# Second batch's attention scores: one float32 product becomes three products of float32r parts, and the parts get single buffers

## The chip, the core and the metric

The program runs on one core of one Trainium2 chip. The metric is the device time of one execution in microseconds (us). Five engines work side by side, each on its own queue of instructions in order: TensorE (PE; its weight loads are listed as PEld), VectorE (DVE), ScalarE (ACT), GpSimd (POOL) and SyncE (SP), which issues most of the transfers. PE runs at one of two granted clocks, 1.2 or 2.4 GHz; the views give the granted share (0.5 or 1.0, or a mean between them).

## The reference, cut to what matters

```python
scores = scale * np.matmul(q, k.transpose(0, 1, 3, 2))     # 4 batches x 12 heads, 448 x 448, depth 64
scores = np.where(mask, -1000000000.0, scores)             # causal
attn = exp(scores - max); attn = attn / (sum(attn) + 1e-9)
x = (attn @ v).transpose(0, 2, 1, 3).reshape(1792, 768)
h = np.maximum(np.maximum(x @ w1, x @ w2), x @ w3)         # first mixture
x = h @ w_out
# then a top-1 mixture of 8 experts: out[token] = gate * relu(x @ w1[e]) @ w2[e]
```

Everything is float32. The choice of an expert by the largest logit depends on the result of the attention, and that is why large products are made from float32r parts: a float32r copy ("high part") of each operand and the float32r rest ("low part"), with the three products high-high, low-high and high-low summed in PSUM.

## The kernel before

Attention works on units. A unit is a pair of heads of one batch, so that six units make a batch: units 0 to 5 are the first batch, 6 to 11 the second, and so on. A unit's queries and keys are transposed so that depth lies on the partitions, the two heads on partitions 0 to 63 and 64 to 127. A block is 112 rows of queries. Since the mask is causal, block i needs 112 * (i + 1) columns of scores: 112, 224, 336 or 448.

The first batch is computed alone (`first_heads`). The second batch is computed in pieces inside `first_mixture`, a loop of 36 steps (m = 0 to 35). In each step, half of one weight tile of the first mixture is decoded from float64 words and split, and nine matmuls of the mixture for the first batch run (`h_half`, L674). The order of the instructions is written out by hand there (`manual_schedule`), so each engine takes its instructions in the order of the program text. One step does this:

- `w_split`: ACT copies the high part of a decoded weight (wp, L649), POOL subtracts the low part (L650), and the pair goes to memory.
- `next(st)`: one piece of the second batch's attention, see below.
- `w_decode`: ACT runs L159 and L160, DVE runs L165, L166 and L167, POOL runs L170.
- `run(late)`: copies and small operations that `next(st)` left for later.
- `h_max` in every second step (ACT L683 or L688, DVE L685 and L689), then `h_half` on PE.

A unit of the second batch takes six steps: three parts p (p = 0 has the blocks of 112 and 224 columns, p = 1 the block of 336, p = 2 the block of 448), two steps each. In a part's first step, `nat_d` multiplies the previous part's probabilities by the values (PE, L332), and `nat_b` takes row maxima and masks (DVE, L301) and the exponential (ACT, L305), for both heads. In its second step, `nat_c` transposes the probabilities (PE, L312) and copies them to SBUF (nh: ACT L318, but DVE L317 for the second head of p = 0), and `nat_a` makes the next part's scores (PE, L284). In the second step of p = 1, `nat_t` also transposes the queries and keys of the next unit (PE, L269); the copies to SBUF (qt by ACT, L271; kt by DVE, L273) are late operations of that step, and stand ahead of the nh copies. The order in that step is thus: PE transposes q and k, transposes the probabilities, makes the scores of p = 2 of the present unit from the present qt and kt; then the next qt and kt are written.

Before the change, qt and kt of even units lie in the buffers with the tags qh and kh, those of odd units in ql and kl. A unit's copies therefore never wait for the unit before. The first of the six transposes of the second batch (unit 6) is made at the end of `first_heads`, where the four buffers are free. The third and fourth batch use the same four tags for their own float32r parts (`at_t`, `at_qk`), with the three products that the change brings to the second batch.

The scores of the second batch are made with float32 operands: each product shows in the trace as two matmul instructions. The two heads' products stand on different rows of the array.

Of the kernel before, what the change touches and what calls it, by code (L numbers as in the profile page):

```python
# [11 lines left out]
F32 = mybir.dt.float32  # L12
F32R = mybir.dt.float32r
# [3 lines left out]
AF = mybir.ActivationFunctionType  # L17
ALU = mybir.AluOpType
# [5 lines left out]
def f32(ap):  # L24
    return ap.bitcast(F32)
# [7 lines left out]
def kernel(  # L33
# [15 lines left out]
    nc = tc.nc  # L49
    P = 128  # L50
    B, H, S, D = q.shape
    NP = H // 2
    CP = 112
# [12 lines left out]
    SCALE = 1.0 / math.sqrt(D)  # L66
# [13 lines left out]
    def prio(n):  # L80
# [13 lines left out]
    att = ph_a.enter_context(tc.tile_pool(name="att", bufs=2))  # L94
# [14 lines left out]
        out=mask[:, S - CP :], in_=mask[:, S - CP :], compare_op=ALU.is_ge, fill=BIG, base=0,  # L109
# [121 lines left out]
    M = [slice(0, D), slice(D, 2 * D)]  # L231
# [19 lines left out]
    NPC = 3  # L251
    qk_t, n_sc, n_pt, n_pth, n_bm = {}, {}, {}, {}, {}

    def blocks(n):
        return ((0, 1), (2,), (3,))[n % NPC]
# [4 lines left out]
    def nat_t(u):  # L260

        rq, rk_ = raws.pop((u, "q")), raws.pop((u, "k"))
        qt, kt = (att.tile([P, S], F32, tag=t + "hl"[u % 2], name=f"{t}t{u}", bufs=1) for t in "qk")
        qk_t[u] = (qt, kt)
        late = []
        for nm, r in (("q", rq), ("k", rk_)):
            pq = ps_t.tile([P, 512], F32, tag="pst", name=f"p{nm}{u}")
            for c in range(NC):
                nc.tensor.transpose(pq[:, c * CP : (c + 1) * CP], r[:, c].rearrange("p j d -> p (j d)"), ident[:CP, :CP])  # L269
            if nm == "q":  # L270
                late.append(lambda pq=pq: nc.scalar.activation(qt, pq[:, :S], AF.Copy, scale=-SCALE))  # L271
            else:
                late.append(lambda pq=pq: nc.vector.tensor_copy(kt, pq[:, :S]))  # L273
        return late

    def nat_a(n):

        qt, kt = qk_t[n // NPC]
        ss = [ps_t.tile([P, 512], F32, tag="pst", name=f"sn{n}_{j}") for j in range(2)]
        off = 0  # L280
        for i in blocks(n):
            L = CP * (i + 1)
            for j, m in enumerate(M):
                nc.tensor.matmul(  # L284
                    ss[j][:CP, off : off + L], lhsT=qt[m, CP * i : CP * i + CP], rhs=kt[m, :L], start=True, stop=True
                )
            off += L
        n_sc[n] = ss

# [62 lines left out]
    def nat_steps():  # L352

        n0, n1 = NPC * NP, NPC * NN
        for n in range(n0, n1):
            u, p = divmod(n, NPC)
            late = []
            if n > n0:
                late += nat_d(n - 1)
            nat_b(n, 0)  # L360
            nat_b(n, 1)
            if p == 2:

                late.append(lambda: at_load(u + 3, "qk") if u + 1 < NN else None)
                late.append(lambda: at_load(u + 1, "v"))
            yield late
            late = []
            if p == 1 and u + 1 < NN:
                late += nat_t(u + 1)
            late += nat_c(n, 0) + nat_c(n, 1)  # L370
            if n + 1 < n1:
                nat_a(n + 1)
            yield late
        yield nat_d(n1 - 1)
# [361 lines left out]
    def first_heads():  # L736
# [9 lines left out]
        for u in range(NP):  # L746
            if u:
                at_p(u - 1, 1, PB[0] + PB[1])
            at_qk(u)
            at_e(u, 0)  # L750
            st = w_decode(u)
            w_raw(u + 2)
            at_e(u, 1, st)
            drain(st)
            if u:
                at_av(u - 1, 1)
                at_x(u - 1, 1)
                at_load(u + 1, "v")
            at_p(u, 0, PB[0] + PB[1])
            at_load(u + 2, "qk")  # L760
            if u + 1 < NP:
                at_t(u + 1)
            else:
                run(nat_t(NP))
            at_n(u)
            if u == 0:
                warm(6)
            at_av(u, 0)
            if u:
                x_split(u - 1)  # L770
            at_r(u)
            at_x(u, 0)
        at_p(NP - 1, 1, PB[0] + PB[1])
        w_split(0)
        nat_a(NPC * NP)
        at_av(NP - 1, 1)
        at_x(NP - 1, 1)
# [71 lines left out]
    def iota_f(shape, pattern, name, base=0, cm=0):  # L849
# [17 lines left out]
        out=tri, in_=tri, compare_op=ALU.is_gt, fill=0.0, base=0, pattern=[[1, P]], channel_multiplier=-1  # L867
# [473 lines left out]
```

## Time and profile before

| | us |
|---|---|
| median of 3 runs | 956.46 |
| lowest and highest | 954.72, 957.21 |
| the profiled execution | 959.22 |
| its span on the core | 957.5 |
| the second batch's scores on PE, first and last start | 79.3 to 204.8 |

Times of rows are microseconds from the start of the span; mean durations marked ns are nanoseconds. The profiled execution took 2.76 us more than the median; 1.7 us of its time lie around the span. The profile gives busy time and share of each engine, a chain of the work that ended last, and for each idle stretch of an engine what ended it. The release of a wait is inferred from semaphore events.

### The profile page before, as it was taken

To read this page: it belongs to the slowest core of one execution; us is meant where nothing else is said; L and a number is where in the kernel's file an instruction comes from. 1 tells how busy PE (TensorE), PEld (TensorE's weight loads), DVE (VectorE), ACT (ScalarE), POOL (GpSimd) and SP (SyncE) were. 2 spreads that over 40 slices of the span, in tenths; PEclk is the share of its full clock that TensorE was granted. 3 is DMA by queue.
4 is the path that set the end of the run, shared out by engine and by line. 5 is a ranking of instruction groups with operands and counts; after the bars stand their busy time and mean duration, and the time that the engine had idled before them with its cause. 6 is when DMAs were issued, how large, how long until landed. Compare 5 with 4: busy or idle time off the path is not lost.

```text
span 957.5 us, 17073 instructions
## 1 busy us (share of the span) xinstructions
PE 929.2 (97%) x5500; PEld 825.3 (86%) x5500; DVE 486.0 (51%) x1287; ACT 458.1 (48%) x1037; POOL 166.9 (17%) x186
## 2 busy tenths in 40 slices
PE   8888999999999999999999998999999999999997
PEld 5666888788989999999999897989989998998996
DVE  4665777866765645455554214541211217749244
ACT  6776667655654656565531003142212216757253
POOL 0114555552321110001020000010010010100101
PEclk9998999999999999999999999899999999999999
DMA  6336787876555532264452992191011116949410
GB/s 147 91 90 199 243 251 247 261 237 184 175 167 160 151 105 63 71 174 147 146 167 83 362 319 80 59 337 38 35 55 46 34 50 223 354 130 382 147 34 26
DMA packets 126354, 150.10 MB, mean 157 GB/s; under 512 B 75934, under 2 KB 93342, under 8 KB 126240
## 3 DMA queue, kind: packets, MB, share of 16 engines
q1 hardware_dynamic: 123200, 135.37, 45.2%
q0 software_dynamic: 3040, 13.41, 4.0%
q8 instruction: 46, 0.75, 0.3%
q14 instruction: 68, 0.56, 0.2%
HBM read 129.85 MB, written 26.77 MB: 164 GB/s over the span
## 4 chain that ended last, share of the span: by engine, by line
PE 85%; DVE 8%; ACT 4%; issue 1%; DMA 1%; POOL 1%; SPq 0%; POOLq 0%; ACTq 0%; DVEq 0%
PE pm L674 24%; PE po L1235 16%; PE ph L1216 16%; PE py L713 9%; PE ss L452 3%; PE pp L511 3%; PE av L547 3%; PE av L535 2%; PE an L332 2%; PE pht L1227 2%; DVE pt L466 1%; PE pxt L1152 1%; ACT pt L471 1%; PE sn L284 1%; PE pr L486 1%
## 5 line engine op out<-in xcount | busy, mean ns | idle before, releaser
L674 PE MATMUL pm<-xh,wp 128*128 128x448 f32 x864 | 272.0, 378 | 0.1
L674 PEld LDWEIGHTS pm<-xh,wp 128*128 128x128 f32 x864 | 162.9, 189 | 23.6 <-issue 10.2
L674 PE MATMUL pm<-xl,wp 128*128 128x448 f32 x432 | 158.8, 368 | 0.0
L1235 PE MATMUL po<-w2h,th 128*128 128x384 f32 x288 | 100.2, 348 | 0.0
L1235 PE MATMUL po<-w2l,th 128*128 128x384 f32 x288 | 97.2, 337 | 0.0
L1235 PE MATMUL po<-w2h,tl 128*128 128x384 f32 x288 | 96.9, 337 | 0.0
L1230 DVE TENSOR_TENSOR tl<-pht,th 128x512 fp32r<-128x512 f32 x36 | 24.9, 690 | 135.1 <-ACT th L1229 88.5
L471 ACT ACTIVATE pt<-pt,bm 112x224 f32<-112x224 f32 (+3 forms) x144 | 75.0, 522 | 26.0 <-DVE bm L466 24.7
L674 PEld LDWEIGHTS pm<-xl,wp 128*128 128x128 f32 x432 | 81.9, 190 | 5.7 <-issue 0.3
L1216 PE MATMUL ph<-w1h,xh 128*128 128x512 f32 x216 | 86.4, 400 | 0.0
L1216 PE MATMUL ph<-w1h,xl 128*128 128x512 f32 x216 | 85.1, 394 | 0.0
L1216 PE MATMUL ph<-w1l,xh 128*128 128x512 f32 x216 | 84.8, 393 | 0.0
L1244 POOL DMA_INDIRECT out_dram<-os,six x18 | 18.4, 1020 | 283.1 <-ACT os L1243 170.9
L466 DVE CUSTOM_DVE_ANT_0 pt<-ss,mask 112x224 f32<-112x224 f32 (+3 forms) x144 | 58.7, 445 | 15.2 <-PE ss L452 11.7
L713 PE MATMUL py<-woh,hth 128*128 128x400 f32 (+1 forms) x168 | 60.6, 360 | 3.6 <-ACT ys L722 3.6
L685 DVE TENSOR_TENSOR g<-pm,g 128x448 f32<-128x448 f32 x48 | 29.8, 620 | 58.3 <-PE pm L674 57.8
L713 PE MATMUL py<-wol,hth 128*128 128x400 f32 (+1 forms) x168 | 58.5, 348 | 0.0
L713 PE MATMUL py<-woh,htl 128*128 128x400 f32 (+1 forms) x168 | 58.4, 347 | 0.0
L1221 ACT ACTIVATE h__7114<-ph 128x512 f32<-128x512 f32 x36 | 21.6, 600 | 70.5 <-PE ph L1216 70.5
L1235 PEld LDWEIGHTS po<-w2h,tl 128*128 128x128 f32 x288 | 54.2, 188 | 0.8
L1235 PEld LDWEIGHTS po<-w2h,th 128*128 128x128 f32 x288 | 54.1, 188 | 0.7
L1235 PEld LDWEIGHTS po<-w2l,th 128*128 128x128 f32 x288 | 54.0, 188 | 0.0
(273 smaller groups left out, 1804.3 us busy)
## 6 DMA issues: line engine op xcount, KB each, us to landing
wp<-wpdram SPq DMA_DIRECT2D x108, 384.0 KB
w1r<-in_moe_w_dram SPq DMA_DIRECT2D x42, 512.0 KB
w2r<-in_moe_w_dram SPq DMA_DIRECT2D x56, 384.0 KB
wpdram<-wp SPq DMA_DIRECT2D x36, 384.0 KB
wxh<-in_moe_w_dram SPq DMA_DIRECT2D x24, 384.0 KB
qraw<-in_q_dram SPq DMA_DIRECT2D x48, 112.0 KB
kraw<-in_k_dram SPq DMA_DIRECT2D x48, 112.0 KB
vraw<-in_v_dram SPq DMA_DIRECT2D x48, 112.0 KB
```

Source lines behind the costliest of these rows:

```text
L452: nc.tensor.matmul(ss, lhsT=l[m, qc], rhs=r[m, :L], start=n == 0, stop=n == len(prods) - 1)
L466: nc.vector.tensor_tensor_reduce(out=pr, in0=ss, in1=mask[:, S - L :], scale=1.0, scalar=3.0e38, op0=ALU.add, op1=ALU.min, accum_out=bm[:, ...
L471: nc.scalar.activation(pr, pr, AF.Exp, bias=bm[:, i : i + 1], scale=-1.0, accum_out=sm[:, j, i : i + 1])
L511: nc.tensor.transpose(pp[:CP, off : off + CP], pt[:, POFF[i] + kt * CP : POFF[i] + (kt + 1) * CP], ident[:CP, :CP])
L547: nc.tensor.matmul(av[:, CP * kt : S], lhsT=vs[:, j, kt, :], rhs=src[:, PTOFF[kt] : PTOFF[kt] + L], start=kt == 0 and src is pth, stop=kt ...
L674: nc.tensor.matmul(pm[:, :S], lhsT=l[:, kk % 3, :], rhs=r, start=kk == 0 and c == 0, stop=kk == KD - 1 and c == 2)
L685: nc.vector.tensor_max(gs["g"], pm[:, :S], gs["g"])
L713: nc.tensor.matmul(pm[:, :w], lhsT=l[:, kk, cs], rhs=r[:, kk, c0 : c0 + w], start=kk == 0 and c == 0, stop=kk == KF - 1 and c == 2,)
L1216: nc.tensor.matmul(pm[a], lhsT=l[:, kk], rhs=r[kk][:, cs], start=kk == 0 and c == 0, stop=kk == KD - 1 and c == 2)
L1221: nc.scalar.activation(h_[:, 512 * a : 512 * a + 512], pm[a], AF.Relu)
L1230: nc.vector.tensor_sub(tl[:, kr], pt, f32(th[:, kr]))
L1235: nc.tensor.matmul(po[a][:, :HN], lhsT=l[:, kk], rhs=r[kk][:, HN * a : HN * a + HN], start=kk == 0 and c == 0, stop=kk == KF2 - 1 and c == 2,)
```

## The change

`nat_t` makes four tiles in place of two: float32r high parts (qh, kh) and low parts (ql, kl) of the scaled queries and the keys. ACT writes qh and then kh; DVE writes ql from the transposed queries and qh, and kl from the transposed keys and kh. Each of the four tags has one buffer, which every unit uses. `nat_a` makes each block's scores with three products per head, summed in PSUM.

```diff
-        qt, kt = (att.tile([P, S], F32, tag=t + "hl"[u % 2], name=f"{t}t{u}", bufs=1) for t in "qk")
-        qk_t[u] = (qt, kt)
+        qh, ql, kh, kl = (att.tile([P, S], F32R, tag=t, name=f"{t}n{u}", bufs=1) for t in ("qh", "ql", "kh", "kl"))
+        qk_t[u] = (qh, ql, kh, kl)
...
-            if nm == "q":
-                late.append(lambda pq=pq: nc.scalar.activation(qt, pq[:, :S], AF.Copy, scale=-SCALE))
-            else:
-                late.append(lambda pq=pq: nc.vector.tensor_copy(kt, pq[:, :S]))
+            def parts(nm=nm, pq=pq):
+                if nm == "q":
+                    nc.scalar.activation(qh, pq[:, :S], AF.Copy, scale=-SCALE)
+                    nc.vector.scalar_tensor_tensor(
+                        out=ql, in0=pq[:, :S], scalar=-SCALE, in1=f32(qh), op0=ALU.mult, op1=ALU.subtract
+                    )
+                else:
+                    nc.scalar.copy(kh, pq[:, :S])
+                    nc.vector.tensor_sub(kl, pq[:, :S], f32(kh))
+
+            late.append(parts)
...
-        qt, kt = qk_t[n // NPC]
+        qh, ql, kh, kl = qk_t[n // NPC]
...
-            for j, m in enumerate(M):
-                nc.tensor.matmul(
-                    ss[j][:CP, off : off + L], lhsT=qt[m, CP * i : CP * i + CP], rhs=kt[m, :L], start=True, stop=True
-                )
+            for c, (l, r) in enumerate(((qh, kh), (ql, kh), (qh, kl))):
+                for j, m in enumerate(M):
+                    nc.tensor.matmul(
+                        ss[j][:CP, off : off + L], lhsT=l[m, CP * i : CP * i + CP], rhs=r[m, :L], start=c == 0,
+                        stop=c == 2,
+                    )
```

## Rows read from the trace of the kernel before

**Rows 1.** The page: busy us of each engine (share of span) xinstructions.
```profile
PE 929.2 (97%) x5500; PEld 825.3 (86%) x5500; DVE 486.0 (51%) x1287; ACT 458.1 (48%) x1037; POOL 166.9 (17%) x186
```
**Rows 2.** Windows, one unit: busy us of PE, PEld, DVE, ACT, POOL; clock; DMA.
```profile
134.84:156.91 22.07, 20.95 (x138) 17.79 (x138) 17.05 (x51) 14.91 (x34) 12.17 (x12) 1.00 0.79 246
```
**Rows 3.** PE's waits, 64 to 222: us in total, times, longest.
```profile
PE an L332 <- DVE nh L317: 5.0, 4, 1.6
```
**Rows 4.** The chain of waits from 130 to 160: start, us, what.
```profile
...
134.84 0.43 DVE nh L317
...
135.31 1.20 PE an L332 x10
...
139.75 0.94 PE sn L284 x4
...
146.48 0.76 PE sn L284 x8
...
153.24 0.80 PE sn L284 x4
...
154.07 0.51 ACT wp L649
...
156.91 0.43 DVE nh L317
...
```
**Rows 5.** The timeline of ACT: start, us, operation, [idle before, releaser].
```profile
...
139.31 0.52 ACT L271 ACTIVATE qt<-pq 128x448 f32<-128x448 f32 x1
139.73 0.76 ACT L318 COPY nh<-pn 112x336 f32<-112x336 f32 x2
...
142.73 1.23 ACT L305 ACTIVATE nt<-nt,nm 112x448 f32<-112x448 f32 x2 [1.83 <-DVE nm L301]
...
153.60 0.56 ACT L688 CAST hth<-g 128x448 fp32r<-128x448 f32 x1 [2.18 <-DVE g L685]
...
```
**Rows 6.** The timeline of DVE, in two units.
```profile
...
97.22 0.62 DVE L273 COPY kt<-pk 128x448 f32<-128x448 f32 x1
97.95 0.62 DVE L301 CUSTOM_DVE_ANT_0 nt<-sn,mask 112x448 f32<-112x448 f32 x1
...
141.54 0.62 DVE L273 COPY kt<-pk 128x448 f32<-128x448 f32 x1
142.07 0.62 DVE L301 CUSTOM_DVE_ANT_0 nt<-sn,mask 112x448 f32<-112x448 f32 x1
...
```
**Rows 7.** The third and fourth batch's parts: count, ns min/median/max, starts, forms.
```profile
...
L421 DVE SCALAR_TENSOR_TENSOR ql<-pq,qh x12: 616/625/625, 222.7 to 458.1; 128x448 fp32r<-128x448 f32 x12
...
L430 ACT CAST kh<-pk x12: 524/529/547, 222.6 to 458.0; 128x448 fp32r<-128x448 f32 x12
L431 DVE TENSOR_TENSOR kl<-pk,kh x12: 614/615/619, 223.3 to 458.7; 128x448 fp32r<-128x448 f32 x12
...
```
**Rows 8.** The timeline of PE, the third batch's scores from three products.
```profile
...
243.73 0.30 PE L452 MATMUL ss<-kh,qh 64*112 64x112 f32 x2
...
244.42 0.32 PE L452 MATMUL ss<-kh,qh 64*112 64x336 f32 x2
...
244.88 0.36 PE L452 MATMUL ss<-kh,qh 64*112 64x448 f32 x2
...
245.28 0.37 PE L452 MATMUL ss<-kl,qh 64*112 64x448 f32 x2
245.58 0.47 PE L674 MATMUL pm<-xh,wp 128*128 128x448 f32 x1
...
```
**Rows 9.** Window of the clock (columns as rows 2), PE's timeline, and the chain.
```profile
91.00:95.00 4.00, 4.00 (x17) 3.74 (x18) 2.74 (x11) 3.61 (x8) 2.22 (x3) 0.58 1.05 373
...
90.99 1.55 PE L332 MATMUL an<-vraw,nh 112*112 112x65 f32 x10 [1.63 <-DVE nh L317]
...
96.98 0.94 PE sn L284 x4
...
```
**Rows 10.** PE's timeline near the end of the second batch.
```profile
...
207.67 1.39 PE L332 MATMUL an<-vraw,nh 112*112 112x65 f32 x12 [0.31 <-ACT nh L318]
...
```

## The prediction, as it was made before the changed kernel ran

> **What bounds the kernel now.** I read the page first [rows 1]: PE is busy 97% of the span, so work taken off PE should count. But that share is a mean over stages, so I looked at the stage the change is in, 79 to 215 us, by windows. A unit of the second batch repeats every 22.07 us, and PE is busy 20.95 us of that [rows 2]: it idles 1.1 us per unit. Next, PE's own waits over the stage [rows 3]: nearly all of that idle time is one wait, by the product with the values (L332) for DVE's copy nh (L317), four times with 5.0 us in total (units 6, 8, 9 and 10). So something other than PE sets the period.
>
> The chain of waits [rows 4] must be read with care here. It runs from DVE's nh at 134.84 along PE to the scores that end at 154.04, jumps to ACT's copy wp at 154.07, and comes back by DVE to nh at 156.91. The jump is a coincidence of 0.03 us: ACT's timeline shows L688 started at 153.60 [rows 5], and 0.47 us from one ACT start to the next is what ACT takes between such copies when it waits for nothing (139.31 to 139.73 is 0.42 [rows 5]). L688 itself waited for DVE. Following ACT and DVE alone, I find each DVE instruction either straight behind the one before it or behind ACT, and each ACT idle stretch ended by DVE: DVE's L301 behind kt at once, 0.53 us after it [rows 6], and ACT's exponential after 1.83 us of waiting for L301 [rows 5]. So DVE and ACT, each in its own order and waiting for each other, form a loop of 22.07 us that PE does not enter. PE is some 1.1 us shorter and waits for the loop once per unit.
>
> **The change, part by part.**
>
> *Scores on PE.* Per unit they now take 0.76 (p = 0), 0.80 (p = 1) and 0.94 us (p = 2) of the chain [rows 4], together 2.50. The three products need no guess, as the third batch makes the same blocks with them [rows 8]: blocks 112 and 224 take 243.73 to 244.42 = 0.69, block 336 takes 0.46, block 448 to the next matmul 0.70. The last pair of 448 takes 0.30 us to the next matmul where 0.20 lies between the earlier ones ((245.28 - 244.88) / 2), so leaving the half-array products costs 0.10. The second batch leaves them three times: 0.79 + 0.56 + 0.70 = 2.05. PE saves 0.45 us a unit (0.24 of it in p = 2), 2.7 us over six units.
>
> The Trainium skill, "FP8 and Floating Point Precision", section TensorE Precision Notes, says that true FP32 takes four passes through the array. By that rule three products would take 3/4 of 2.50 and save 0.63 us a unit, 3.8 in all; the trace shows two matmul instructions for a float32 product, and the third batch's rows give the smaller 0.45.
>
> *Copies.* ACT: qt becomes qh (same size), and kh is added, 0.53 us, 0.42 from start to start. DVE: kt (0.62) goes, ql and kl come, 0.62 each [rows 7]; from start to start DVE needs 0.53 [rows 6]. Loop cost: 0.53 us on DVE per unit, unless something else is later.
>
> *Single buffers.* This is the new wait. qh of the next unit may be written only when p = 2 of the present unit is through PE, because its products read qh. ACT has it first in that step's late work; behind it in ACT's order stand kh, two nh copies and wp, behind ql on DVE stand kl and then L301. In the unit of [rows 4] the p = 2 scores end at 140.69, and 0.24 sooner after the change: 140.45. qh starts near 140.49 in place of 139.31, kh 140.91, nh 141.33 and 141.70, end 142.1. PE wants nh after nine mixture matmuls (2.02 us by the same chain), at 142.47, so 0.4 us of cover remain. DVE: ql at 141.54 in kt's place (qh has ended at 141.01), kl at 142.07, L301 at 142.60. ACT's 1.83 us of idle time before the exponential swallows its own delay. Result: the loop grows by 0.53 us, not by more.
>
> Where PE is late the cover is gone. With E for the end of the p = 2 scores: qh from E + 0.04, ql from E + 0.60, kl + 0.53, L301 at E + 1.66. Unit 6 is such a case: before, L301 started at 97.95, at the end of scores that began at 96.98 and took 0.94 [rows 6, 9]; after, E = 97.68 and L301 at 99.34. That unit costs 1.39 us.
>
> *The clock.* Why was PE late there? It had waited 1.63 us for nh, and then the granted clock was 0.58 over 91 to 95 us [rows 9], which means mostly 1.2 GHz. From that wait's end at 90.99 to the end of the scores PE took 97.92 - 90.99 = 6.93 us; at 2.4 GHz the same work takes 140.69 - 135.31 = 5.38 [rows 4]. So a fall costs PE 1.55 us. In units 8 to 10 the wait is 1.1 us [rows 3] and the clock stays at 1.00 [rows 2]. The change lengthens just this wait: PE arrives 0.45 us sooner, nh comes 0.53 later, 2.1 us in all; for unit 7, which has no wait now, 1.39 + 0.45 = 1.8. These are longer than the wait before the fall. Where the clock falls, E = 140.45 + 1.55 = 142.00 and L301 starts at 143.66 where it started at 142.07: 1.59 us lost, not 0.53.
>
> *What costs nothing.* The first `nat_t` at the end of `first_heads` finds its buffers free. The extra DVE and ACT work there delays nobody: PE has value products to run meanwhile. Without that cover it would cost 0.5 us, once. The load and issue order of SP does not change. Memory is that of the third batch's tags, and no new tile is added.
>
> **The sum**, against the profiled 959.22. Unit 6: +1.39. Units 7, 8, 9: 0.53 each if the clock holds, 1.59 if it falls; I take two falls of three, 0.53 + 2 * 1.59 = 3.71. Unit 10's parts come after the last wait of PE for nh; from there PE, ACT and the loads stand close together (PE waits 0.31 us for ACT at 207.67 [rows 10]), so up to 0.69 us of PE's saving of the last products comes back; I take 0.3. Total +4.8: 964.0 in the profiled execution's terms, 956.46 + 4.8 = 961.3 as a median. After 215 us PE has little idle time, so the delay reaches the end.
>
> **The rivals.**
> - *The clock holds*: 1.39 + 3 * 0.53 = 2.98, less 0 to 0.69: 958.8 to 959.4. For it: a wait of 1.1 us brought no fall [rows 2, 3]. Against: 1.63 did [rows 9], and these are longer.
> - *PE is the bound after all* (faster, or no slower): the jump in the chain at 154.07 is real, and each unit is PE's 2.50 us of scores shorter by 0.45. Time 956.46 - 2.7 = 953.8, by the four-pass rule above 952.7. It decides where ACT and DVE have 0.53 us of free time per unit that I have not seen; then the copies cost nothing. Against it: PE idles 1.1 us per unit already, and shortening it lengthens that.
> - *The delay is absorbed*: waits for loads near 190 to 207 us take it up, 956.5. For it: ACT's and PE's idle times there; against: the loads' issues wait for the same ACT and DVE work.
> - *All boundaries fall, and unit 10's too*: 1.39 + 3 * 1.59 + 1.55 - 0.3 = 7.4, 963.9.
>
> **Chances.** Some falls: 0.50. Clock holds: 0.25. PE bound: 0.08. Absorbed: 0.10. All fall: 0.07. A measurement of this kernel can tell about 0.3% (2.9 us) from no change. Falls are all slower by more (0.57); of "the clock holds" 0.10 is, since 2.3 to 2.98 straddles that bound; the rest, absorbed, and half of PE bound are no change (0.29); half of PE bound is faster (0.04). So faster 0.04, same 0.29, slower 0.67. The range leaves out PE bound and the worst of the last case: 956.3 to 963.6. The forecast's own range is 960.2 (one fall of the three) to 962.3 (all three).
>
> **What would show it.** Right: the wait of L332 for nh in units 7 to 10 grows from 0 or 1.1 us to 1.5 or more; the period from nh to nh grows from 22.07 to 22.6 or, with a fall, 23.6; ACT's qh starts right behind PE's scores of block 448; L301 follows kl. The granted clock shows falls between 110 and 185 us that are not there before. Scores take 2.05 us a unit. Wrong: the period stays at 22.07 or less (then ACT and DVE were no loop), the clock stays at 1.0 in spite of waits of 2 us, or the three products take more than the third batch's rows say. What I cannot see from before: whether instructions that are planned automatically behind the second batch are ordered otherwise, which could move the end either way.

## The result, and the profile after

The changed kernel takes 966.76 us (median of 4 runs, 965.70 to 967.44) beside 956.84 for the kernel before: ratio 1.0104, 95% interval 1.0085 to 1.0122. That is 9.9 us slower; 4.8 were forecast, and the range ended at 963.6. The profiled execution took 965.70 (span 963.9), 6.5 us more than that of before (the profiled execution of before was 2.4 us above the median of its kernel, that of the changed kernel 1.1 below); a second profile of the same kernel, further down, has a span of 967.1. Line numbers of the attention are about ten higher after the change: L293 makes the scores, L311 the maxima, L315 the exponential, L342 the product with the values, L327 and L328 the nh copies.

First the windows of the changed kernel from one nh copy of part p = 0 to the next (columns as in [rows 2]): the units that begin at 88, 111, 136 and 160 us.

```profile
88.51:111.11 22.60, 20.94 (x146) 18.22 (x146) 17.58 (x51) 15.37 (x35) 12.22 (x12) 1.00 0.87 273
111.11:136.50 25.39, 24.06 (x146) 21.15 (x146) 17.67 (x51) 15.35 (x35) 12.19 (x12) 0.87 0.70 214
136.50:160.34 23.84, 22.49 (x146) 19.70 (x146) 17.67 (x51) 15.37 (x35) 12.22 (x12) 0.93 0.74 228
160.34:182.94 22.60, 20.91 (x146) 18.25 (x146) 17.59 (x51) 15.35 (x35) 12.22 (x12) 1.00 0.82 257
```

The first and the last of them have a clock of 1.00 and take 22.60 us where [rows 2] has 22.07: the 0.53 us that DVE's additional instruction was to cost. The two others have clocks of 0.87 and 0.93 and take 2.8 and 1.2 us more again. The window of 111 to 119 shows 0.57, mostly 1.2 GHz. In what follows a fall is a stretch in which the granted clock is 0.50, that is 1.2 GHz.

PE's waits in the stage, 64 to 235 us, answer to [rows 3]:

```profile
PE an L342 <- DVE nh L327: 6.2, 5, 1.7
PE an L342 <- ACT nh L328: 2.3, 6, 0.6
```

The wait for DVE's nh is there in all of five units. Beside it stands a wait for ACT's nh that was not forecast. The longest wait stands before the unit from 88 us, which had no fall; the unit from 160 us had stops of 0.23 and 1.12 us and no fall either:

```profile
88.97 1.20 PE L342 MATMUL an<-vraw,nh 112*112 112x65 f32 x10 [1.72 <-DVE nh L327]
159.28 0.41 PE L342 MATMUL an<-vraw,nh 112*112 112x65 f32 x2 [0.23 <-ACT nh L328]
160.81 1.20 PE L342 MATMUL an<-vraw,nh 112*112 112x65 f32 x10 [1.12 <-DVE nh L327]
```

The timelines of ACT, DVE and PE in the unit from 160 us answer to [rows 5, 6, 8]:

```profile
166.09 0.55 ACT L273 ACTIVATE qhn<-pq 128x448 fp32r<-128x448 f32 x1 [1.21 <-PE sn L293]
166.53 0.53 ACT L278 CAST khn<-pk 128x448 fp32r<-128x448 f32 x1
...
168.77 1.23 ACT L315 ACTIVATE nt<-nt,nm 112x448 f32<-112x448 f32 x2 [0.62 <-DVE nm L311]
```

```profile
167.05 0.62 DVE L274 SCALAR_TENSOR_TENSOR qln<-pq,qhn 128x448 fp32r<-128x448 f32 x1
167.59 0.61 DVE L279 TENSOR_TENSOR kln<-pk,khn 128x448 fp32r<-128x448 f32 x1
168.12 0.61 DVE L311 CUSTOM_DVE_ANT_0 nt<-sn,mask 112x448 f32<-112x448 f32 x1
```

```profile
165.18 0.46 PE L293 MATMUL sn<-khn,qhn 64*112 64x448 f32 x2
165.48 0.37 PE L293 MATMUL sn<-khn,qln 64*112 64x448 f32 x2
165.68 0.37 PE L293 MATMUL sn<-kln,qhn 64*112 64x448 f32 x2
165.98 0.47 PE L684 MATMUL pm<-xh,wp 128*128 128x448 f32 x1
...
181.90 0.41 PE L342 MATMUL an<-vraw,nh 112*112 112x65 f32 x2 [0.59 <-ACT nh L328]
183.41 0.80 PE L342 MATMUL an<-vraw,nh 112*112 112x65 f32 x6 [1.11 <-DVE nh L327]
```

ACT writes qh only when PE has finished with the old one, and waits 1.21 us for it; its later wait for DVE shrinks from 1.83 to 0.62, so that the delay goes no further. DVE runs L167, ql, kl and L311 without a gap. The scores of block 448 take 0.80 us from start to start, not 0.70: their first pair takes 0.30 to the next start, where the third batch, which comes to block 448 from other half-array products, took 0.20. PE now stops twice in the product with the values, for ACT's nh and then for DVE's, as the last two lines show for the end of the unit.

### The profile page after: what moved, and what is told of

Its sections match the earlier page's. It is cut to its first block, busy times and chain, and to the rows that moved or that the text cites. A ratio compares the mean times of both kernels' runs of the same rounds, so it can differ in the third digit from the quotient of the medians.

```text
span 963.9 us, 17191 instructions
## 1 busy us (share of the span) xinstructions
PE 930.4 (97%) x5548; PEld 829.7 (86%) x5548; DVE 490.1 (51%) x1293; ACT 460.8 (48%) x1043; POOL 166.6 (17%) x186
## 4 chain that ended last, share of the span: by engine, by line
PE 78%; DVE 10%; ACT 6%; DMA 3%; issue 2%; POOL 1%; SPq 0%; ACTq 0%; POOLq 0%; DVEq 0%
PE pm L684 21%; PE po L1245 15%; PE ph L1226 15%; PE py L723 9%; PE ss L462 3%; PE pp L521 3%; PE av L557 3%; PE pht L1237 2%; PE av L545 2%; DVE pt L476 1%; ACT nt L315 1%; PE pxt L1162 1%; ACT pt L481 1%; DVE wxl L167 1%; PE an L342 1%
## 5 line engine op out<-in xcount | busy, mean ns | idle before, releaser
L684 PEld LDWEIGHTS pm<-xh,wp 128*128 128x128 f32 x864 | 163.8, 190 | 19.9 <-issue 4.5
```

The costliest lines, as they stand in the source:

```text
L684: nc.tensor.matmul(pm[:, :S], lhsT=l[:, kk % 3, :], rhs=r, start=kk == 0 and c == 0, stop=kk == KD - 1 and c == 2)
```

## The experiments

The runs of the kernel before beside them have medians of 957.57 (31 runs, first four experiments), 957.54 (17, next four) and 957.16 (23, last three). Single executions of the kernel before spread from 952.6 to 961.8 us, so totals settle little below 2 us, and the period, from one DVE row of a unit to the same row of the next, is the finer measure. A ratio weighs all executions and differs a little from that of the two medians. The rows of the periods stand together behind the first eight.

**1. Two buffers for the high parts.**

```diff
+        if u % 2:
+            a_ = att.tile([P, 2, S], F32R, tag="vs", name=f"an{u}", bufs=1)
+            qh, kh = a_[:, 0], a_[:, 1]
+            ql, kl = (att.tile([P, S], F32R, tag=t, name=f"{t}n{u}", bufs=1) for t in ("ql", "kl"))
+        else:
             qh, ql, kh, kl = ...
```

> The changed kernel, but odd units keep their high parts qh and kh in a second pair of buffers, so that ACT no longer waits for PE's scores before it writes them. Loop theory (the cost is DVE's additional instruction per unit in a loop of DVE and ACT, made worse where the clock falls): period 22.6 us without a fall, still 3 to 8 us slower than before, 960 to 965. Wait theory (the cost is the wait for the single buffers): back to 956 to 958.

Only the high parts of odd units get a second pair of buffers; the low parts keep one each. Measured: 965.28 us, ratio 1.0064 (1.0040 to 1.0089). Period 22.58 without a fall: the wait for single buffers is not what lengthens the loop. Each of the two units with a fall (one over 159.8 to 163.2) took 23.08, only 0.5 more, where the changed kernel has 1.2. That 0.5 is in part the low parts' single buffer: DVE's ql waits for PE's scores.

```profile
165.78 0.62 DVE L279 SCALAR_TENSOR_TENSOR qln<-pq,qhn 128x448 fp32r<-128x448 f32 x1 [0.38 <-PE sn L298]
```

The profiled total (966.47) stayed high for another reason: the last unit took 24.3 us (before: 19.9), with PE waiting 3.0 us once for an nh copy on ACT. Three of the eight executions took only 960.0 to 961.5; there is no profile of those.

**2. One buffer each, with float32 products.**

```diff
-        qt, kt = (att.tile([P, S], F32, tag=t + "hl"[u % 2], name=f"{t}t{u}", bufs=1) for t in "qk")
+        qt, kt = (att.tile([P, S], F32, tag=t + "h", name=f"{t}t{u}", bufs=1) for t in "qk")
```

> The kernel before, float32 products and two copies, but one buffer each for qt and kt: the wait alone. Loop theory: ACT waits 1.2 us for PE but has 1.8 us to spare, so the period stays 22.07 where the clock holds, and the time is 956 to 958.5. Wait theory: most of the 10 us, 962 to 967.

Measured: 956.35 us, ratio 0.9994 (0.9977 to 1.0011), period 22.04. None of its units has a fall, and there the single buffers cost nothing by themselves. The wait theory does not hold; what single buffers cost in a unit with a fall this run does not show.

**3. The copies alone.**

```diff
+                if u > NP:
+                    xa = att.tile([P, 512], F32R, tag="mn", name=f"xa{u}", bufs=1)[:, :S]
+                    xd = att.tile([P, 512], F32R, tag="rb", name=f"xd{u}", bufs=1)[:, :S]
+                    late.append(lambda pq=pq: nc.scalar.copy(xa, pq[:, :S]))
+                    late.append(lambda pq=pq: nc.vector.tensor_sub(xd, pq[:, :S], f32(xa)))
                 late.append(lambda pq=pq: nc.vector.tensor_copy(kt, pq[:, :S]))
```

> The kernel before, with one more ACT copy and one more DVE subtraction in the place of kh and kl for units 7 to 11, into buffers that nobody reads; products and buffers as before. Loop theory: period 22.6, five times 0.53 = 2.65 us at least, more with falls of the clock: 959.5 to 964. Wait theory and a theory that blames the three products on PE: 956.5 to 957.5.

Measured: 959.27 us, ratio 1.0016 (1.0000 to 1.0032), period 22.56 (22.60 in a unit with a fall at 88.6, 23.9 in one with a fall of 6.8 us from 133.0). The period is that of the changed kernel; the total is just below the 959.5 to 964 that the loop asked for. The copies alone are a part of the 9.9 us, not most of it.

**4. kt on ACT in the kernel before.**

```diff
-                late.append(lambda pq=pq: nc.vector.tensor_copy(kt, pq[:, :S]))
+                late.append(lambda pq=pq: nc.scalar.copy(kt, pq[:, :S]))
```

> The kernel before, with kt copied by ACT in place of DVE. Loop theory: DVE's turn is 0.53 us shorter, ACT has 1.8 us to spare there, so the period falls to 21.54 and the time by 2.65 us, to 953.5 to 955. If PE is the bound: no change, 956.8.

Measured: 958.10 us, ratio 1.0000 (0.9981 to 1.0020). The period fell to 21.52 as the loop theory says, so DVE's turn does set it. The total did not follow, and 953.5 to 955 was missed: in the profile the first of the four units took 22.27 us as before, the other three gained 3 * 0.54 = 1.6, and the last unit, with a wait of 1.5 us for an nh copy on ACT and a fall at 195.1, took 21.9 us, not 19.9, which gives back all of it.

**5. The changed kernel again**, unedited.

> The changed kernel once more, unedited, for a second profile and more runs beside the next three. If the falls of the clock make its size: period 22.60 us in each unit without a fall, 1.2 to 2.8 us more in each with one, at other units than in the first profile, and executions with a lower mean clock are the longer ones. Loop theory alone: 22.60 in every unit, and 959 to 960 in all. Median 964 to 968.

Measured: 967.95 us (6 runs), ratio 1.0109 (1.0082 to 1.0135). Each of the four units had a fall this time: the periods are 23.80, 23.77, 23.79 and 23.78. The mean granted clock over its six executions is 0.9825, over the 17 of the kernel before 0.9912. Its three longest executions (968.78 to 970.27) have 0.979 to 0.981, the three others 0.984 to 0.986, as was expected if falls make its size.

**6. One product of the high parts.**

```diff
-            for c, (l, r) in enumerate(((qh, kh), (ql, kh), (qh, kl))):
-                for j, m in enumerate(M):
-                    nc.tensor.matmul(..., lhsT=l[...], rhs=r[...], start=c == 0, stop=c == 2)
+            for j, m in enumerate(M):
+                nc.tensor.matmul(..., lhsT=f32(qh)[...], rhs=f32(kh)[...], start=True, stop=True)
```

> The changed kernel with its four copies and single buffers, but the scores as one float32 product of the two high parts (the two low parts are made and not used, so the scores leave out the low terms). Loop theory with falls: as slow as the changed kernel, 963 to 967, period 22.60. If the three products on PE are the cost: 958 to 960.

Measured: 963.61 us, ratio 1.0067 (1.0045 to 1.0089); periods 23.98, 22.55, 23.96, 23.97. The scores leave out the low terms here. With the float32 product on PE, four copies and single buffers give the changed kernel's loop, falls and all, and 6.1 of the 10.4 us that the changed kernel lost beside it. How the other 4.3 us come with the three products is not shown; this profile lacks the late fall near 240 us, of which more below. Experiment 3 has nearly the same copies, old buffers, and 1.0016; experiment 2 the single buffers without the copies, and 0.9994. Neither alone costs what both do together.

**7. More work on PE.**

```diff
+            if n % NPC == 1:
+                for _ in range(6):
+                    for j, m in enumerate(M):
+                        nc.tensor.matmul(..., lhsT=qh[...], rhs=kh[...], start=True, stop=True)
             for c, (l, r) in enumerate(((qh, kh), (ql, kh), (qh, kl))):
```

> The changed kernel with twelve more matmuls on PE per unit (the high-high product of block 336 six times more for both heads, overwritten by the real one), 1.0 us of PE work where PE waits 1.7 us a little later. Clock theory: PE's wait for nh is 0.7 us, falls in the second batch become rare, 3 to 5 us faster than the changed kernel in spite of more work: 961 to 964. PE theory: 6 us slower than the changed kernel, 972.

Measured: 963.35 us, ratio 1.0063 (1.0039 to 1.0088), 4.6 us less than the unedited kernel beside it, with 1.0 us more of matmuls in every unit. All four periods are 22.60 to 22.62, with a clock of 1.00 from one nh to the next, and PE waits once a unit, 0.8 to 1.1 us. None of the other theories on record makes the kernel faster by giving PE more. In the last unit the clock fell at 191.9 us, and that unit took 24.3.

**8. The nh copy on ACT, in the changed kernel.**

```diff
-        if j and n % NPC == 0:
-            return [lambda: nc.vector.tensor_copy(pth[:, o0 : o0 + w], pp[:CP, :w])]
         return [lambda: nc.scalar.copy(pth[:, o0 : o0 + w], pp[:CP, :w])]
```

> The changed kernel with the nh copy of part p = 0, second head, on ACT in place of DVE. Loop theory: DVE is 0.42 us shorter per unit, period 22.18; PE no longer waits for DVE's nh at the end of DVE's turn, so its idle time is split, and falls become rarer: 2 to 6 us faster than the changed kernel, 961 to 965. If DVE's turn sets nothing: unchanged.

Measured: 960.37 us, ratio 1.0035 (1.0017 to 1.0053), 7.6 us less than the changed kernel. Period 22.19, as the loop theory gives (22.60 - 0.42), and no fall in the four units: the clock is 1.00 from 89 to 178 us, with stops of PE of 0.6 to 0.9 us.

The DVE rows from which the periods come, two consecutive units each, in the order of the experiments: two buffers, one buffer each, copies alone, kt on ACT, changed kernel again, one product, more work on PE, nh on ACT. Start, us, operation.

```profile
113.35 0.50 DVE L332 COPY nh<-pn 112x336 f32<-112x336 f32 x1
135.93 0.50 DVE L332 COPY nh<-pn 112x336 f32<-112x336 f32 x1
```
```profile
109.37 0.50 DVE L317 COPY nh<-pn 112x336 f32<-112x336 f32 x1
131.41 0.50 DVE L317 COPY nh<-pn 112x336 f32<-112x336 f32 x1
```
```profile
109.66 0.50 DVE L322 COPY nh<-pn 112x336 f32<-112x336 f32 x1
132.22 0.50 DVE L322 COPY nh<-pn 112x336 f32<-112x336 f32 x1
```
```profile
135.19 0.50 DVE L317 COPY nh<-pn 112x336 f32<-112x336 f32 x1
156.71 0.50 DVE L317 COPY nh<-pn 112x336 f32<-112x336 f32 x1
```
```profile
137.25 0.50 DVE L327 COPY nh<-pn 112x336 f32<-112x336 f32 x1
161.04 0.50 DVE L327 COPY nh<-pn 112x336 f32<-112x336 f32 x1
```
```profile
134.84 0.50 DVE L326 COPY nh<-pn 112x336 f32<-112x336 f32 x1
158.80 0.50 DVE L326 COPY nh<-pn 112x336 f32<-112x336 f32 x1
```
```profile
114.23 0.50 DVE L334 COPY nh<-pn 112x336 f32<-112x336 f32 x1
136.83 0.50 DVE L334 COPY nh<-pn 112x336 f32<-112x336 f32 x1
```
```profile
133.70 0.50 DVE L311 CUSTOM_DVE_ANT_0 nt<-sn,mask 112x336 f32<-112x336 f32 x1
155.89 0.50 DVE L311 CUSTOM_DVE_ANT_0 nt<-sn,mask 112x336 f32<-112x336 f32 x1
```

What a fall does is seen in the second profile of the changed kernel, in the unit from 137 us: the window of the clock, then PE, ACT and DVE.

```profile
138.00:143.00 5.00, 5.00 (x27) 4.59 (x27) 3.70 (x12) 3.66 (x8) 3.21 (x4) 0.66 0.79 239
```
```profile
136.29 0.41 PE L342 MATMUL an<-vraw,nh 112*112 112x65 f32 x2 [0.20 <-ACT nh L328]
137.81 1.37 PE L342 MATMUL an<-vraw,nh 112*112 112x65 f32 x10 [1.11 <-DVE nh L327]
```
```profile
144.63 0.55 ACT L273 ACTIVATE qhn<-pq 128x448 fp32r<-128x448 f32 x1 [2.76 <-PE sn L293]
```
```profile
145.21 0.62 DVE L274 SCALAR_TENSOR_TENSOR qln<-pq,qhn 128x448 fp32r<-128x448 f32 x1 [1.09 <-ACT qhn L273]
```

PE stops 0.20 and 1.11 us, the clock falls at 138.7, the scores of block 448 come late, ACT holds qh for 2.76 us, and DVE, the engine that sets the period, stands idle for 1.09 us behind ACT. The loop of DVE and ACT does not contain PE while the clock holds; a fall pulls PE into it through the single buffer. In the next unit PE has the lead again, stops again for 1.12 us, and the clock falls again at 162.6. This is not so every time: in the first profile the unit from 136 us had a fall at 138.9, PE then stopped 0.23 and 1.12 us, and no fall followed.

The Trainium skill, "TensorE: Matmul & The Clock Gate", section "HAM oscillation — how this bites in real kernels", tells of a kernel whose waits for transfers between bursts of matmuls bring the clock down each time anew. The second profile agrees with that pattern (four units of four, 23.8 us each), the first only in part (two of four); the waits here are for copies, and shorter than those of the page. With more work on PE none of four units had a fall (22.6 us each).

**9. The nh copy on ACT, in the kernel before** (edit of experiment 8).

> The kernel before, with the nh copy of part p = 0, second head, on ACT in place of DVE. Loop theory: DVE's turn is 0.42 us shorter, period 21.65, four to five units: 1.7 to 2.1 us faster, unless the last unit gives it back as it did for kt on ACT; PE's one wait of 1.1 us is gone. 953.5 to 957.5. If DVE's turn sets nothing: 957.5.

Measured: 957.19 us, ratio 1.0013 (0.9991 to 1.0035), period 21.68. The period follows; a gain in the total is not to be told from none.

```profile
132.62 0.50 DVE L301 CUSTOM_DVE_ANT_0 nt<-sn,mask 112x336 f32<-112x336 f32 x1
154.30 0.50 DVE L301 CUSTOM_DVE_ANT_0 nt<-sn,mask 112x336 f32<-112x336 f32 x1
```

**10. The nh copy and kt on ACT, in the kernel before** (edits of experiments 4 and 8).

> The kernel before, with both that nh copy and kt on ACT. Loop theory: 0.95 us off DVE's turn, 21.1, close to PE's own 20.95, so PE nearly never waits: 952 to 957. If ACT becomes the bound in its place: 957.5 or more.

Measured: 953.75 us, ratio 0.9971 (0.9953 to 0.9990), faster than both kernels. Its profile has PE busy in every part of a unit:

```profile
129.31:150.42 21.11, 21.11 (x141) 18.07 (x140) 16.09 (x48) 15.67 (x36) 12.18 (x12) 1.00 0.86 256
```

**11. Both cures in the changed kernel** (edits of experiments 7 and 8).

> The changed kernel with the nh copy on ACT and the twelve additional matmuls: both cures. Loop theory: period 22.18. Clock theory: waits are split and short already, so the additional matmuls win nothing more and may cost up to 1 us a unit where PE is close to the loop: 959 to 964.

Measured: 962.42 us, ratio 1.0057 (1.0041 to 1.0073), period 22.20, no better than the nh copy on ACT alone (1.0035). With no fall in the four units of experiment 8 to take away, the additional matmuls gained nothing here.

## Why the prediction was right in kind and wrong in size

*The bound.* Right. DVE and ACT set the period, and it moves with the number of DVE's instructions: 21.11 with two fewer copies on DVE (there PE is busy throughout, so that PE may be the bound by then), 21.52 and 21.68 with one fewer, 22.04 to 22.07 as before, 22.56 to 22.60 with one more. PE's saving bought nothing.

*Scores on PE.* Mis-sized: 0.45 us a unit was forecast. From start to start the three parts take 0.79, 0.65 and 0.80, together 2.24 for 2.05. The cost of entering the half-array products was left out for p = 1 and p = 2; for p = 0 the third batch's rows begin with such an entry, and its 0.79 came out. Before, the three parts take 2.45 from start to start (0.76, 0.75, 0.94), so PE saves 0.21 us a unit.

*Copies.* Right: 0.53 us a unit without a fall.

*Single buffers.* Right that they cost nothing while the clock holds (experiment 2), and that the cover goes where PE is late (ACT's wait of 2.76 us, DVE's of 1.09).

*The clock.* Right in how a fall costs and in the price of one: 1.59 us lost in place of 0.53 was forecast for a unit, that is a period of 23.66; 23.8 was measured. What was to bring the falls came out otherwise. A single wait of 1.8 to 2.1 us for DVE's nh was forecast in units 7 to 10, longer than the 1.63 before the fall in the kernel before. That wait stayed at 1.11 to 1.12 us, a second of at most 0.6 us, for ACT's nh, stands ahead of it, and falls came all the same; after 1.72 us in unit 6 of the first profile none came. That unit took 22.60 us, 0.3 more than before, where 1.39 more was taken as certain.

*The sum* is the step that failed, in three terms. With the rows of nh, the second profile (span 967.1) against that of before (957.5) splits so: the first nh comes 0.8 us sooner (89.7 for 90.4, with the clock falling at other times in `first_heads`), the next four units take 95.1 for 88.5 us (+6.7), the last one 22.5 for 19.9 (+2.5), and all that follows 759.8 for 758.6 (+1.2): 9.6. In the first profile these are -2.0, +6.0, +1.0 and +1.4: 6.5 between the two profiles.

- Four units: 1.39 + 3.71 = 5.1 was forecast with two falls of three beside unit 6's. In the second profile there was a fall in each, four of four: 6.7. In the first there were two, one of them twice as long: 6.0. I had half seen this (the last rival). That one fall makes the next likely, since PE waits again after it, is argued and not shown; the forecast treated them as separate chances, and unit 6's as certain.
- The last unit: -0.3 was forecast, since PE's saving was to come back. It took 1.0 us longer in the first profile (without a fall there) and 2.5 in the second (with one at 186.5). Part of that comes back: from the nh that begins the last unit to PE's L200 after the batch (below) the kernel before takes 52.4 us, the changed kernel 52.5 and 54.4. So the loss is 0.1 us without a fall and 2.0 with one; a fall is not hidden.
- After the second batch: nothing was forecast. In both profiles of the changed kernel the clock falls once more, at 237.9 and 241.1 us, and from L200 to the first product of `y_half` it takes 101.8 us in both, where the kernel before and all experiments, none with such a fall, take 100.3: 1.5 us. L200 in the kernel before, and in the first and second profile of the changed kernel:

```profile
231.31 1.51 PE L200 MATMUL pg<-wg,wt 128*128 128x16 f32 x12 [0.40 <-DVE g L685]
235.34 1.51 PE L200 MATMUL pg<-wg,wt 128*128 128x16 f32 x12 [0.72 <-DVE g L695]
239.21 1.51 PE L200 MATMUL pg<-wg,wt 128*128 128x16 f32 x12 [0.69 <-DVE g L695]
```

The mean clocks say the same over more executions: 2 * (1 - 0.9825) * 966 = 34 us at 1.2 GHz, beside 2 * (1 - 0.9912) * 956 = 17 in the kernel before, as much more as five falls like the one from 159.8 to 163.2. Over the first four executions the mean is 0.985, which gives 29 us.

*Rivals.* "PE is the bound", "absorbed" and "the clock holds" fell. "All boundaries fall" came nearest, at 963.9 with a chance of 0.07. Some later instructions are ordered otherwise, as was held possible: a few of ACT's and DVE's in the decoding of weights change places around the last unit. What that costs was not measured.

*Open.* Why the same stops are followed by a fall in one unit and not in another. The last unit takes 19.8 to 26.8 us over all these kernels. There the decoding of w_out, ordered automatically, shares ACT and DVE with the second batch; in the changed kernel two buffers, more work on PE and the nh copy on ACT show a wait of 2.3 to 3.1 us for ACT's nh in it. That its order makes the difference was not tried. Nor was it tried why the clock falls near 240 us in the changed kernel only.

## What to carry to other kernels

A busy share of 97% did not make PE the bound: in this stage two engines waiting for each other in order set the period, and 0.53 us on one of them per turn counted in full while 0.2 us off PE counted for nothing. An engine whose clock can fall after it has stood still must be costed twice: a longer wait of it may cost more than the wait, above all if something late on it, here a single buffer, then holds the engines that do set the period. Before adding an instruction to a chain of this kind, look for one that can leave it: kt and one nh copy on ACT gained 3.4 us.

## What the runs showed of the hardware that was not expected

Twelve needless matmuls a unit, 1.0 us of work, made the changed kernel 4.6 us faster (967.95 to 963.35), and in its profile the granted clock stays at 1.00 for four units. The length of PE's stop alone does not tell a fall. In the two profiles of the changed kernel PE stopped 1.1 to 1.8 us in all at each of ten places, and a fall came within 2 us in seven; none came after 1.72, after 0.23 and 1.12, and after 0.59 and 1.11 us. Single stops of 0.8 to 1.1 us, in the kernel before and in experiments 2 and 7, were followed by none. A pair of half-array products that follows full-height ones took 0.30 us to the next start, against 0.20 for the pairs behind it.
